# Second half of x by block transposes, the residual's moves from ScalarE's queue, and the rest group ahead of the last late blocks

## The chip, the cores and the metric

The kernel runs on one core of a Trainium2 chip. A core has a matrix engine (TensorE, PE in the profile, with its weight loads as PEld), a vector engine (VectorE, DVE), a scalar engine (ScalarE, ACT), a general engine (GpSimd, POOL) and a sync engine (SyncE, SP). SP and ACT can both issue transfers (DMAs), and each engine works off its own instructions in order and waits for the others by semaphores. The metric is the device time of one execution in microseconds (us); smaller is better.

## The reference

Two blocks follow each other on 8 batches of 576 tokens, all in 32-bit floats. The first is attention with 8 heads of width 64 in which only scores within `tau` of the row's maximum are kept. The second is a mixer: a small network over the tokens, added to x, then one over the channels, added to that.

```
# q, k, v: (8, 8, 576, 64); w_tok1 (576, 256), w_tok2 (256, 576), w_ch1 (512, 1536), w_ch2 (1536, 512)
scores = scale * q @ k^T
scores = where(scores >= max(scores) - tau, scores, -1e9)
attn = exp(scores - max(scores)); attn /= sum(attn) + 1e-9
x = (attn @ v), heads side by side: (8, 576, 512)

h  = relu(x^T @ w_tok1) @ w_tok2          # over tokens
u  = x + h^T
h2 = relu(u @ w_ch1) @ w_ch2              # over channels
out = u + h2
```

## The kernel before

**How the work is cut.** A batch is called a row here, 0 to 7. Its 8 heads are 4 pairs, and two pairs side by side (a "quad", 4 heads, 256 of the 512 channels) are worked through in nine units of 128 query rows. Two units make a score round (`scores_of_two`, L848), after which DVE takes the maximum (`top`, L865), POOL makes the bias (`shift`, L871), ACT masks and takes exponentials (`mask`, L881, and `exps`, L891), DVE inverts the sums (L277, L278), POOL scales (`scale`, L286), DVE transposes in blocks of 32 by 32 (`turn_blocks`, L316), and four DMAs per unit put the blocks in place (`move`, L328). After three units PE multiplies by v (`values`, L366 and L371). Its result is copied to `xT` (L375), which holds x with the channels on the partitions.

**x with tokens on the partitions.** The token network needs x the other way round, in `x_sb`. For rows 1 to 7 this is done in two ways. The first quad, ready half a row early, goes through `early_x`: two DVE block transposes (L398) into a tile `xs`, then four DMAs of 128 KB on SP (L411), then the last 64 tokens in the same manner (L405, L418). The second quad goes through PE: `turn_x` (L441) transposes four 128x128 blocks into a PSUM bank, twice, and a third time for the last 64 tokens; ACT or DVE copies each bank to `x_sb` (L445). The columns that the DMA way leaves are in another order of blocks, and `tok1` (L460) reads the first quad through a rearranged view.

**The token network.** `tok1` multiplies `w1` by x, in two steps per row, ReLU follows (L470 or L473); `tok2` (L478) multiplies by `w2`, and `add_x` (L489) adds into `xT`.

**The channel network.** Each row has two groups of 256 tokens and a rest of 64. The list `NOW` says how many groups of a row run during the attention: both of row 0, one each of rows 1 to 6, none of row 7. Such a group has 12 first-layer steps (`ch1`, L1058, ReLU at L1063 on ACT or L1066 on DVE) and, but for row 0's first, seven products in place of eight (`make_seven`, L982), the sums for which are taken on DVE and POOL. The residual u is needed there with the tokens on the partitions: `turn_u` (L1043) transposes it in blocks on DVE, and `move_u` (L1050) issues 4 moves of two DMAs each, on SP's queue, into `ut`. Seven groups do so.

**What is put off.** The other groups run after the attention, as "late" blocks of 512 tokens (class `Late`, products at L1430): two groups per block, the last of these being both groups of row 7, and as a fifth block the eight rests of 64 tokens. Rows 0 to 6 are kept in device memory meanwhile (`spill`, L537) and loaded again (L1447). A late block has seven products at each of two levels, so that its second half is a net of sums on DVE and POOL. For each of two halves m (128 tokens of either group t), a fifth product (`x5`) is added into two of the four output parts. The outputs go to memory by `store` (L1455), four stores per block, all on SP; in the block of rests each store is two DMAs of 64 tokens.

**What sets the order.** All instructions are placed by a planner written in the kernel (`Scheduler`). An operation has an engine, a cost in us, dependencies and a rank; the planner keeps a clock for each engine, places what can start first, and the engines then keep this order. Two PSUM banks serve everything but the scores until the attention ends, eight after that. A DMA is modelled with its issue time, its size, and at most eight in flight. A score round of row 1 and later is held back while the planned PE work of the token and channel networks is behind `planned_at`: the more is subtracted there (`KEEP`, for the second to last row `KEEP_LAST`), the earlier the round may run.

The few lines that steer this before the change:

```
KEEP, KEEP_LAST = 24.0, 26.0
...
return total + part * (k - 2) / (UB // 2) - (KEEP_LAST if row == B - 2 else KEEP)
...
groups.append([(b, 2 * GR, REST) for b in range(B)])
```

## Time and profile before

| what | us |
|---|---|
| median of 3 runs (1227.75 to 1229.17) | 1227.9 |
| the profiled execution | 1229.4 |
| its span, first to last instruction | 1227.6 |
| attention with rows 0 to 7 woven in | to about 862 |
| five late blocks (products L1430) | 864 to 1220 |

The profile is of one execution. Its span leaves out 1.8 us that the device time holds around it. A row of the attention takes about 98 us in the middle of the kernel. Between 272 and 770 us, PE is busy 99% of the time, DVE 73%, ACT 56%, POOL 35%, and the 16 transfer engines some 70 to 78%. The granted TensorE clock is 0.997 of full speed in the mean.

A group line of the page names the code line, the engine, the operation, output and input, how often, the busy time and the mean of one; a wait line names who waited for whom. PE's matmuls overlap, so a matmul's own duration is longer than the step from one start to the next: a first-layer step of the channel network (8 records) takes 1.75 us from start to start.

### The profile page before, as it was taken

How to read it: one execution, taken by the hardware profiler on the slowest of the kernel's cores; microseconds unless marked ns; L12 is line 12 of the kernel's file. 1: busy time of each engine (PE TensorE's matmuls, PEld its weight loads, DVE VectorE, ACT ScalarE, POOL GpSimd, SP SyncE). 2: the span in 40 equal slices, each digit the busy share in tenths (PEclk: the TensorE clock that was granted, in tenths of full speed). 3: DMA queues.
4: the chain of work that ended last, by engine and by line, in shares of the span. 5: the costliest groups of instructions: out<-in, count | busy, mean ns of one | idle time of the engine just before them, and what ended most of it. 6: DMA issues, size and time to landing. Idle time of an engine off the chain costs nothing.

```text
span 1227.6 us, 21546 instructions
## 1 busy us (share of the span) xinstructions
PE 1199.0 (98%) x7769; PEld 972.6 (79%) x7769; DVE 877.8 (71%) x1406; ACT 572.6 (47%) x1279; POOL 365.7 (30%) x568
## 2 busy tenths in 40 slices
PE   9888999999999999999999999999999999999996
PEld 8655788777777777876877777788899898999986
DVE  6798996777778668776867766843767575766756
ACT  6987863555663665574555456530211212121220
POOL 3666552333343423332433323411001010110101
PEclk9999999999999999999999999999999999999999
DMA  8656867767778757877767687661211202020101
GB/s 145 140 121 163 234 169 169 153 145 179 175 161 185 174 124 178 182 158 168 161 153 168 151 183 152 151 165 34 52 35 47 58 18 53 1 69 1 54 17 35
DMA packets 325370, 149.76 MB, mean 122 GB/s; under 512 B 223824, under 2 KB 318032, under 8 KB 325264
## 3 DMA queue, kind: packets, MB, share of 16 engines
q1 hardware_dynamic: 323392, 148.17, 52.9%
q8 instruction: 62, 1.02, 0.3%
q10 hardware_dynamic: 1872, 0.21, 0.1%
q14 instruction: 44, 0.36, 0.1%
HBM read 47.32 MB, written 13.50 MB: 50 GB/s over the span
## 4 chain that ended last, share of the span: by engine, by line
PE 85%; DVE 2%; DMA 0%; ACT 0%; issue 0%; SPq 0%; DVEq 0%
PE bank L1430 28%; PE bank L1058 12%; PE bank L982 11%; PE sc L848 10%; PE bank L371 8%; PE bank L460 5%; PE bank L478 5%; PE bank L366 3%; PE bank L1073 2%; DVE mx L865 1%; PE bank L441 0%; DVE us L946 0%; DVE g L1066 0%; DMA lk<-in_k_dram 0%; ACT e L881 0%
## 5 line engine op out<-in xcount | busy, mean ns | idle before, releaser
L881 ACT ACTIVATE e<-sc,bias 128x576 f32<-128x576 f32 x288 | 194.3, 742 | 173.1 <-POOL bias L871 171.9
L286 POOL TENSOR_SCALAR e<-e,rr 128x576 f32<-128x576 f32 x288 | 216.6, 769 | 189.3 <-DVE rr L278 187.8
L891 ACT ACTIVATE e<-e,ntau 128x576 f32<-128x576 f32 x288 | 220.8, 780 | 0.2
L865 DVE TENSOR_REDUCE mx<-sc 128x2 f32<-128x1152 f32 x144 | 188.1, 1348 | 40.5 <-PE sc L848 39.8
L316 DVE STREAM_TRANSPOSE T<-e 128x1152 f32<-128x1152 f32 x126 | 171.0, 1365 | 31.0 <-POOL e L286 21.8
L1058 PE MATMUL bank<-xT,wc 128*128 128x256 f32 x768 | 177.1, 383 | 1.9 <-ACT g L1063 0.9
L848 PE MATMUL sc<-kT,qT 64*128 64x192 f32 (+1 forms) x1920 | 165.5, 333 | 1.0 <-ACT e L881 1.0
L1058 PEld LDWEIGHTS bank<-xT,wc 128*128 128x128 f32 x768 | 143.0, 190 | 28.9 <-issue 4.4
L848 PEld LDWEIGHTS sc<-kT,qT 64*128 64x128 f32 (+1 forms) x1920 | 138.4, 176 | 31.2 <-issue 19.3
L371 PE MATMUL bank<-eT,lv 128*64 128x384 f32 (+1 forms) x1024 | 135.1, 406 | 0.0
L371 PEld LDWEIGHTS bank<-eT,lv 128*64 128x64 f32 x1024 | 73.7, 137 | 50.5 <-issue 44.3
L871 POOL TENSOR_SCALAR bias<-mx,toff 128x2 f32<-128x2 f32 x144 | 39.3, 273 | 193.1 <-DVE mx L865 186.0
L946 POOL TENSOR_TENSOR us<-us,late_x 128x256 f32<-128x256 f32 x14 | 13.1, 934 | 219.9 <-DVE us L946 156.9
L982 PE MATMUL bank<-wc,g 128*128 128x256 f32 x336 | 77.8, 381 | 0.0
L478 PE MATMUL bank<-w,a 128*128 128x192 f32 (+1 forms) x256 | 74.4, 425 | 1.2 <-DVE xT L489 0.7
L460 PE MATMUL bank<-x_sb,w 128*128 128x256 f32 x320 | 73.0, 383 | 0.7 <-DVE x_sb L445 0.5
L982 PEld LDWEIGHTS bank<-wc,g 128*128 128x128 f32 x336 | 63.1, 190 | 12.8 <-issue 2.5
L460 PEld LDWEIGHTS bank<-x_sb,w 128*128 128x128 f32 x320 | 59.8, 190 | 10.9 <-issue 1.1
L478 PEld LDWEIGHTS bank<-w,a 128*128 128x128 f32 x256 | 43.6, 192 | 22.5 <-issue 6.4
L1430 PE MATMUL bank<-t,w1s 128*128 128x256 f32 x240 | 60.8, 379 | 0.0
L946 DVE TENSOR_TENSOR temps<-bank,temps 128x256 f32<-128x256 f32 x60 | 25.3, 422 | 49.5 <-PE bank L1430 47.1
L1430 PE MATMUL bank<-t,wc 128*128 128x256 f32 x240 | 59.2, 379 | 0.0
(175 smaller groups left out, 1820.0 us busy)
## 6 DMA issues: line engine op xcount, KB each, us to landing
eT<-T SPq DMA_DIRECT2D x504, 144.0 KB, 3.0
w2s<-in_moe_w_ch_dram SPq DMA_DIRECT2D x24, 512.0 KB, 4.2
lk<-in_k_dram SPq DMA_DIRECT2D x122, 72.0 KB, 2.9
ut<-us SPq DMA_DIRECT2D x136, 64.0 KB, 2.1
lq<-in_q_dram SPq DMA_DIRECT2D x120, 72.0 KB, 3.1
out_dram<-us SPq DMA_DIRECT2D x32, 256.0 KB, 2.1
lv<-in_v_dram SPq DMA_DIRECT2D x112, 72.0 KB, 2.5
spill<-xT SPq DMA_DIRECT2D x6, 640.0 KB, 4.0
```

Of the source, the lines that this page charges most:

```text
L286: nc.gpsimd.tensor_scalar(out=eh, in0=eh, scalar1=rr[:, h : h + 1], scalar2=1.0, op0=ALU.mult, op1=ALU.mult)
L316: nc.vector.transpose(out=T.rearrange("p a (c x) -> p c a x", c=NK), in_=e.rearrange("p (c a x) -> p c a x", c=NK, a=4))
L371: nc.tensor.matmul(to[r], lhsT=lv[:, j, :], rhs=e[j], start=False, stop=(c == NI - 1), skip_group_check=True)
L460: nc.tensor.matmul(to, lhsT=w1[:, t, P * m : P * m + P], rhs=x(t), start=(t == 0), stop=(t == NT - 1), skip_group_check=len(products) > 1,)
L478: nc.tensor.matmul(bank[:, n * i : n * i + n], lhsT=hidden[b][:, m, P * c : P * c + P], rhs=w2[:, m, lo : lo + n], start=(m == 0), stop=(m ...
L848: nc.tensor.matmul(sc[h][rows, f, HT * k : HT * k + HT], lhsT=qT[r, cols], rhs=kT[r, HT * f : HT * f + HT], start=True, stop=True, skip_gr ...
L865: nc.vector.tensor_reduce(out=mx[:, h], in_=sc[h][:, :, 0 : 2 * HT].rearrange("p f (k x) -> p k f x", k=2), axis=AX.XY, op=ALU.max)
L881: nc.scalar.activation(out=eh, in_=part[h], func=AF.Prelu, bias=bias[:, h], scale=SCALE, alpha=STEEP)
L891: nc.scalar.activation(out=eh, in_=eh, func=AF.Exp, bias=ntau, accum_out=rs[:, h, 0:1])
L982: nc.tensor.matmul(bank[:, 0:HD], lhsT=x[:, j, :], rhs=y[:, j, :], start=j == 0, stop=j == HJ - 1)
L1058: nc.tensor.matmul(bank[:, 0:n], lhsT=wc1[:, j, c, :], rhs=uT[:, c, GR * i : GR * i + n], start=(c == 0), stop=(c == NCC - 1))
L1430: nc.tensor.matmul(to, lhsT=l, rhs=r, start=start and x == 0, stop=x == len(pairs) - 1, skip_group_check=not start)
```

## The change

- `early_x` takes the first pair `c0` as an argument and is called for the second quad of rows 1 to 7 as well, without its last 64 tokens. `turn_x` has only these 64 tokens left in those rows. `tok1` reads the second quad's main part through a rearranged view too. The moves are ranked ahead of the other transfers in the planner.
- `move_u` issues on ACT's queue, with rank 3 in place of 1 and a modelled issue time of 0.55 us.
- `KEEP` and `KEEP_LAST` go from 24 and 26 us to 14 and 20.
- The block of rests is put in the third place of the five; row 7's block is the last.
- In the last block (`ends`), the fifth products come after the inner ones, their addends are prepared by an addition on POOL or DVE, and the stores of the second group (t = 1) go to ACT's queue.

```
-    def early_x(b):
+    def early_x(b, c0):
...
-                in_=xT[:, c, 0:MAIN].rearrange("q (t r a) -> q t a r", t=NI, a=4),
+                in_=xT[:, c0 + c, 0:MAIN].rearrange("q (t r a) -> q t a r", t=NI, a=4),
...
-                out=x_sb[:, 0:NI, 32 * HQ * i : 32 * HQ * i + 32 * HQ],
+                out=x_sb[:, 0:NI, P * c0 + 32 * HQ * i : P * c0 + 32 * HQ * i + 32 * HQ],
...
-        for t, n in [(t, n) for t in range(0, NI, n)] + [(NI, 1)]:
+        for t, n in [(t, n) for t in range(0, NI, n) if not b] + [(NI, 1)]:
...
-    KEEP, KEEP_LAST = 24.0, 26.0
+    KEEP, KEEP_LAST = 14.0, 20.0
...
+        moved = [sched.op("sp", 1.2, lambda i=i: move_main(i), turns + before, -1 if c0 else 0, dmas=(1, 131, 0.69)) for i in range(4)]
+        if not c0:
+            last = sched.op("dve", 0.35, turn_rest, moved, 2)
...
-                    nc.sync.dma_start(
+                    eng.dma_start(
                         out=s["ut"][:, m, k, :], in_=s["us"][32 * k : 32 * k + 32, m]
...
-                moved = [sched.op("sp", 1.2, lambda k=k, m=move_u: m(k), (turn,), 1, dmas=(nt, 64, 0.69)) for k in range(4)]
+                moved = [sched.op("act", 1.2, lambda k=k, m=move_u: m(k, nc.scalar), (turn,), 3, dmas=(nt, 64, 0.55)) for k in range(4)]
...
+        while late_due and key_op("V", rank_of_group(late_due[0], HQ, 2)).end is not None:
+            make_early(late_due.pop(0), HQ)
...
-    groups.append([(b, 2 * GR, REST) for b in range(B)])
+    groups.insert(2, [(b, 2 * GR, REST) for b in range(B)])
...
+            ends = self.n == len(groups) - 1
+            for m in range(0 if ends else 2):
                 x5 = plain(lambda m=m: sum_place(0, m), lambda: w2s[:, 0], [s1[m]])
...
+                if ends:
+                    b11 = on_pool(lambda eng, m=m: add(old(1, 1, m), old(1, 1, m), four(w7_of(m)), eng), [u3] + moved[m])
+                    x5 = plain(lambda m=m: sum_place(0, m), lambda: w2s[:, 0], [s1[m]] + small_used[0] + small_used[1][:1])
+                    q11 = put_mid("dve", 0.42, lambda bank, m=m: add(four(o(1, 1, m)), four(bank), old(1, 1, m)), x5, [x5, b11])
+                    q01b = put_leave("dve", 0.42, lambda bank, m=m: add(o(0, 1, m), bank[:, 0:HD], o(0, 1, m)), x5, [x5, q11, q01b])
...
+                    if ends and t:
+                        x = sched.op("act", 0.53, lambda m=m, t=t, rows=rows: self.store(2 * t + m, rows(), nc.scalar), deps, 1)
```

More of the change, by code (lines that the diff above doesn't have):

```diff
@@ L454, in tok1 @@
             else:
-                first = lambda t: x_sb[:, t, 0 : P * HQ].rearrange("p (i c d) -> p c i d", i=4, c=HQ)
-                products = [(slice(0, P * HQ), first), (to_cols, lambda t: x_sb[:, t, to_cols])]
+                blocks = lambda t, c0: x_sb[:, t, P * c0 : P * c0 + P * HQ].rearrange("p (i c d) -> p c i d", i=4, c=HQ)
+                products = [
+                    (slice(0, P * HQ), lambda t: blocks(t, 0)),
+                    (to_cols, lambda t: blocks(t, HQ) if t < NI else x_sb[:, t, to_cols]),
+                ]
             for at, x in products:
@@ L927, with make_early @@
     early = {}
-    def make_early(b):
-        turn_main, turn_rest, move_main, move_rest = early_x(b)
-        have = [key_op("X", rank_of_group(b, 0, g)) for g in range(3)]
-        free = early.get(b - 1, []) + [x for k, x in keyed.items() if k[0] == "tok" and k[1] == b - 1 and len(k) == 3]
+    def make_early(b, c0=0):
+        turn_main, turn_rest, move_main, move_rest = early_x(b, c0)
+        have = [key_op("X", rank_of_group(b, c0, g)) for g in range(3)]
+        free = early.get(b if c0 else b - 1, []) + [x for k, x in keyed.items() if k[0] == "tok" and k[1] == b - 1 and len(k) == 3]
         turns = [sched.op("dve", 1.1, lambda c=c: turn_main(c), have + free, 2) for c in range(HQ)]
         before = [x for k, x in keyed.items() if k[0] == "tok" and k[1] == b - 1 and len(k) == 3 and x.first_layer]
-        moved = [sched.op("sp", 1.2, lambda i=i: move_main(i), turns + before, 0, dmas=(1, 131, 0.69)) for i in range(4)]
-        last = sched.op("dve", 0.35, turn_rest, moved, 2)
-        moved += [sched.op("sp", 0.6, lambda i=i: move_rest(i), [last] + before, 0, dmas=(1, 16, 0.6)) for i in range(4)]
-        early[b] = moved
-        xreads.setdefault(b, []).extend(turns + [last])
+        moved = [sched.op("sp", 1.2, lambda i=i: move_main(i), turns + before, -1 if c0 else 0, dmas=(1, 131, 0.69)) for i in range(4)]
+        if not c0:
+            last = sched.op("dve", 0.35, turn_rest, moved, 2)
+            moved += [sched.op("sp", 0.6, lambda i=i: move_rest(i), [last] + before, 0, dmas=(1, 16, 0.6)) for i in range(4)]
+            turns.append(last)
+        early[b] = early.get(b, []) + moved
+        xreads.setdefault(b, []).extend(turns)
     def side2(k, n):
@@ L1046, in turn_u, with move_u @@
                     )
-            def move_u(k, s=s):
+            def move_u(k, eng, s=s):
                 for m in range(nt):
-                    nc.sync.dma_start(
+                    eng.dma_start(
                         out=s["ut"][:, m, k, :], in_=s["us"][32 * k : 32 * k + 32, m]
@@ L1267, in make_round @@
                 if t // GU == 2:
-                    (rows_due if p0 == NP - 2 else early_due).append(b)
-    rows_due, early_due = [], []
+                    (late_due if p0 else early_due).append(b)
+                    if p0:
+                        rows_due.append(b)
+    rows_due, early_due, late_due = [], [], []
     def planned_at(row, k):
@@ L1448, in load, with store @@
                 at += n
-        def store(self, t, rows):
+        def store(self, t, rows, eng=None):
             at = 0
@@ L1454, in store @@
                 if first < last:
-                    nc.sync.dma_start(
+                    (eng or nc.sync).dma_start(
                         out=out[b, lo + first - at : lo + last - at, :], in_=rows[first - P * t : last - P * t]
@@ L1613, in make_second @@
                 s4[m] = sched.op("dve", 0.96, lambda m=m: sub(a(0, 1, m), a(0, 1, m), sum_place(1, m)), [s2[m], x2[m]], 2)
-            for m in range(2):
+            ends = self.n == len(groups) - 1
+            for m in range(0 if ends else 2):
                 x5 = plain(lambda m=m: sum_place(0, m), lambda: w2s[:, 0], [s1[m]])
@@ L1626, in make_second @@
                 u2 = on_pool(lambda eng, m=m: add(w6_place(m), w6_place(m), p1_place(m), eng), w6[m] + [c1[m]], rank=2)
-                q01a = on_pool(lambda eng, m=m: add(four(o(0, 1, m)), four(o(0, 1, m)), old(0, 1, m), eng), w3[m] + [y5b[m]])
+                q01a = on_pool(lambda eng, m=m: add(four(o(0, 1, m)), four(o(0, 1, m)), old(0, 1, m), eng), w3[m] + [y5b[m]] + moved[m])
                 q01b = on_pool(lambda eng, m=m: add(o(0, 1, m), o(0, 1, m), w6_place(m), eng), [q01a, u2])
@@ L1631, in make_second @@
                 q10b = on_pool(lambda eng, m=m: add(o(1, 0, m), o(1, 0, m), w7_of(m), eng), [q10a, u3])
-                q11 = on_pool(lambda eng, m=m: add(o(1, 1, m), o(1, 1, m), w7_of(m), eng), [y5[m], u3])
+                if ends:
[3 more added lines that the diff above has]
+                    q01b = put_leave("dve", 0.42, lambda bank, m=m: add(o(0, 1, m), bank[:, 0:HD], o(0, 1, m)), x5, [x5, q11, q01b])
+                else:
+                    q11 = on_pool(lambda eng, m=m: add(o(1, 1, m), o(1, 1, m), w7_of(m), eng), [y5[m], u3])
                 self.outs[m] = [q00, q01b, q10b, q11]
@@ L1635, in make_second @@
                     count = 2 if len(groups[self.n]) > 2 else 1
-                    self.stores[m].append(
-                        sched.op("sp", 0.6, lambda m=m, t=t: self.store(2 * t + m, self.us[m][:, t].rearrange("q a x -> q (a x)")), deps, 1, dmas=(count, 256 // count, 0.6))
-                    )
+                    rows = lambda m=m, t=t: self.us[m][:, t].rearrange("q a x -> q (a x)")
+                    if ends and t:
+                        x = sched.op("act", 0.53, lambda m=m, t=t, rows=rows: self.store(2 * t + m, rows(), nc.scalar), deps, 1)
+                    else:
+                        x = sched.op("sp", 0.6, lambda m=m, t=t, rows=rows: self.store(2 * t + m, rows()), deps, 1, dmas=(count, 256 // count, 0.6))
+                    self.stores[m].append(x)
                 all_second += self.outs[m]
```

## The prediction

> **What bounds the kernel now.** I read the page's busy shares and its chain of waits first, then the busy time by stretches, then the waits of TensorE (PE), then single stretches of the timeline around the edited steps.

> ```profile
> PE 1199.0 (98%) x7769; PEld 972.6 (79%) x7769; DVE 877.8 (71%) x1406; ACT 572.6 (47%) x1279; POOL 365.7 (30%) x568
> ...
> PE 85%; DVE 2%; DMA 0%; ACT 0%; issue 0%; SPq 0%; DVEq 0%
> ```

> The chain that ends last is PE work. The stretches (columns: length, then busy us of PE, weight loads, DVE, ACT, POOL, clock, DMA share, GB/s) say where PE is not full:

> ```profile
> 0.00:120.00 120.00, 106.14 (x837) 78.59 (x838) 97.12 (x169) 99.73 (x209) 68.60 (x111) 0.99 0.66 140
> 120.00:260.00 140.00, 137.69 (x978) 110.20 (x977) 113.20 (x160) 87.83 (x192) 58.30 (x82) 1.00 0.75 178
> ...
> 680.00:820.00 140.00, 139.93 (x908) 109.08 (x904) 101.64 (x136) 72.91 (x160) 47.10 (x78) 1.00 0.72 161
> ...
> 1150.00:1200.00 50.00, 50.00 (x257) 44.63 (x255) 30.54 (x60) 11.72 (x30) 2.43 (x3) 1.00 0.15 43
> 1200.00:1228.00 28.00, 17.95 (x144) 16.99 (x142) 17.91 (x43) 1.59 (x6) 4.93 (x7) 0.90 0.17 38
> ```

> From 120 to 1200 us PE idles about 5 us in all. Only the start (14 us idle) and the end (10 us idle) hold more. So a microsecond of PE work removed in the middle is a microsecond gained, as long as nothing new makes PE wait; and the last 28 us are a stage of their own, where DVE and the stores set the end.

> **The transposes that go.** Rows 1 to 7 lose two PE transpose steps each (four 128x128 transposes into one bank, L441, then a copy, L445). Two of them in the timeline:

> ```profile
> 630.35 0.66 PE L441 MATMUL bank<-ident,xT 128*128 128x128 f32 x4
> 630.84 1.89 PE L1058 MATMUL bank<-xT,wc 128*128 128x256 f32 x8
> 632.57 0.60 PE L441 MATMUL bank<-ident,xT 128*128 128x128 f32 x4
> 633.46 1.99 PE L1058 MATMUL bank<-xT,wc 128*128 128x256 f32 x8 [0.29 <-DVE g L1066]
> ```

> A step's price is the time from its start to the next instruction's start, 0.49 and 0.89 us here (the second holds a bank wait of 0.29). Eight such steps, near 333, 531, 631 and 826 us, sum to 4.85 us with the waits and 4.28 without: 0.61 or 0.54 each. Fourteen steps are 8.5 or 7.5 us; I take **-8.0**. The built order of the changed kernel has 56 transposes fewer and every other PE instruction in the same number, so this part is certain. Fourteen copies of 0.58 us (ACT) or 0.68 us (DVE) go too, off the path.

> **What brings x instead.** Per row two block transposes on DVE and four 128 KB moves on SP. The first quad already does this, so its rows price it:

> ```profile
> 280.98 0.56 DVE L375 COPY xT<-bank 128x384 f32<-128x384 f32 x1 [1.02 <-PE bank L371]
> ...
> 282.94 2.16 DVE L398 STREAM_TRANSPOSE xs<-xT 128x512 f32<-128x512 f32 x2
> ```
> ```profile
> 285.74 2.87 SPq L411 DMA_DIRECT2D x_sb<-xs  x4
> ```
> ```profile
> DMA to landing us min/median/max: 2.8/3.3/4.3
> ```

> From the end of the values product (280.9) to the last landing (285.7+2.9+3.3 = 291.9) is 11.0 us. What lies in front of the first layer's second half in the changed order, from the row's last values product on, with the durations of before (ch1 step L1058 1.75, score round 2.15 or 2.3, seven-product L982 2.6, remaining transposes 0.3, values 3.3, and the first layer's own first half 2.2): row 1 has 11.6 us, row 4 12.4, row 7 10.2, rows 2, 3, 5 and 6 at least 17. In row 7 the attention is over and DVE and SP stand free, so its chain is 0.6+2.2+2.5+3.3 = 8.6 us. So x arrives about as it is needed: I take **+1.0** for all rows. Lower bound 0. Upper bound: a maximum pair lies in front on DVE (2.6 us, L865) and eight eT moves on SP (5 us). Then the chain is 18.6 us in rows 1 and 4, and 11.2 in row 7, where only DVE's 2.6 can be: 7.0, 6.2 and 1.0 late, 14 us. The 11.0 us already hold some such queueing (1.4 us before the turn, 0.6 before SP), so I don't count both in both rows and use +9. DVE gains 14 x 1.11 = 15.6 us in some 740 us where it is 73% busy, and SP 28 x 0.63 = 17.7 us.

> [...]

> **The residual's moves.** Seven groups issue four moves of two DMAs each (L1050): 56 issues of 0.60 us leave SP and go to ACT. SP wins 34 us and, with the 18 added, is 16 us lighter; nothing on PE waits for SP's issue time alone, so no gain. ACT, 56% busy there, is held while it issues: the five ACT issues at the start took 0.36 to 0.58 us each, SP's 0.60, so a block of eight is about 4.8 us. Each issue also waits for the DVE turn and for transfers further up. Queued behind it on ACT are the ch1 ReLUs that free PE's two banks and the masks of the next round. In the built order three ch1 steps (5.2 us) beside such a block in row 0 drain through DVE, and a score round (2.15) follows: 7.4 us of cover for 4.8. I take **+1.5** in all; bounds 0 and +7 (1 us in each group). If the cover were gone, a block would cost its 4.8 us.

> **The lead.** The planner's lead falls from 24 to 14 us, so more of the older rows' products run before a score round. That moves PE work, it makes none; as five idle us are spread over 1080, I put 0 (-1 to +3).

> **The late blocks.** The rest group now comes third. Its eight loads (8 x 0.6 us issue, 3.2 us landing) come a group ahead, and a late group lasts about 70 us: 0. The last group is now a pair of whole blocks, and its two fifth products (six 128x256 matmuls, 2.6 us each) run at the very end. The end today:

> ```profile
> 1215.90 0.83 PE L1430 MATMUL bank<-late_x,hidden_b 128*128 128x128 f32 x6
> ...
> 1216.57 0.83 PE L1430 MATMUL bank<-wc,ga 128*128 128x128 f32 x6
> ...
> 1218.01 6.79 SPq L1455 DMA_DIRECT2D out_dram<-us  x8
> ...
> 1219.02 0.91 PE L1430 MATMUL bank<-wc,hidden_b 128*128 128x128 f32 x6 [1.61 <-DVE us L946]
> ...
> 1221.84 0.42 DVE L946 TENSOR_TENSOR us<-us,late_x 128x256 f32<-128x256 f32 x1
> ```

> PE waits 1.6 us for DVE, DVE ends at 1222.26, and SP, which issues eight 128 KB stores at 0.6 us, starts the last at 1224.2; it lands 2.4 us later and the span ends 1.0 after that. Now: without the 5.2 us of fifth products the inner chain comes 5.1 us earlier (DVE had 5.3 us idle in it), PE reaches 1217.4 at 1212.3, does the first fifth product to 1214.9, the last inner one to 1215.6, the second fifth one to 1218.2. DVE's adds, 1.5 us more of them, run along to 1218.0; the two on the last bank end at 1219.3, 3.0 earlier than 1222.3. One 256 KB store on each queue is then left (2.1 us to landing), so 1.9 us of queue and 0.3 of landing go too: **-5.1**. Bounds: -1.5 if DVE can't come forward and only the store queue's gain stays, -6.5 if the first gap closes too.

> **Sum.** -8.0 + 1.0 + 1.5 - 5.1 = -10.6 us. The profiled execution took 1229.4 us (span 1227.6 and 1.8 around it): 1218.8. The median of the runs, 1227.9, lies 1.5 below that, so **1217.3 us**.

> **Rivals.**
> - *x comes late.* The 11 us chain meets DVE and SP as busy as in the bound above: +9 for +1, about 1225. For it: row 1 and 4 have only 0.6 and 1.4 us to spare, and SP issues about 0.6 us apiece almost without pause. Against it: four of seven rows have 6 us more.
> - *The end is DVE's.* DVE is busy 17.9 of the last 28 us, ends after PE, and gets 1.5 us more; the fifth products then only fill waits, the tail gives -1.5: about 1221. Against it: its 5.3 idle us just before.
> - *Slower: ACT is held by its DMA issues.* One block of eight per group, seven times. Past 7.4 us of cover, an issue of 1.3 us (SP's slowest for these moves was 1.6) makes a block 10.4 us and PE loses 3.0 us seven times, 21 in place of 1.5: about 1237. It decides from 12.1/7 = 1.7 us lost per group, an issue of (7.4+1.7)/8 = 1.14 us. For it: the issues wait on transfers already in flight. Against it: SP's median for the very same moves, 0.60.
> - That the transposes stay is excluded by the built order.

> **How the numbers follow.** Forecast 0.55, x late 0.20, the end 0.15, ACT held 0.10. Below 0.2% (2.5 us), which is about what this kernel's timing can tell from no change, lies only an edge of x late. Faster 0.87, same 0.03, slower 0.10. The range 1211 to 1227 reaches from both best ends (-8.5, -6.5, 0, -1) to x late; it leaves out ACT held and the edges. The forecast's own range is 1212 to 1221.

> **What would show it.** PE's matmul records fall by 56, L441's 128x128 group from 72 to 16. PE's waits between 120 and 860 us stay under 8 us; a wait of the first layer (L460 before) for a DMA, or of ch1 for an ACT ReLU, would name the first or third rival. The last matmul ends near 1218.2 - 8.0 + 2.5 = 1212.7 with no PE gap over 1 us ahead of it, then comes one store per queue, and the span ends within 5 us. It is wrong if PE's idle time in the attention grows by more than 8 us.

## The result, and the profile after

The changed kernel takes 1242.1 us in the median of six runs (1238.3 to 1243.5), the kernel before 1227.9 on the same chips: 1.0105 times as long (95% interval 1.0086 to 1.0124), some 13 us slower. The profiled execution took 1238.3 us, the fastest of the six, with a span of 1236.5: the trace holds 9 us of the loss. The six runs go with the granted clock, 0.995 of full speed in the two fastest and 0.991 to 0.993 in the others.

The page's busy shares, and the first line of its chain of waits:

```profile
PE 1195.5 (97%) x7713; PEld 967.7 (78%) x7713; DVE 887.6 (72%) x1414; ACT 567.6 (46%) x1271; POOL 371.1 (30%) x568
...
PE 71%; DVE 5%; DMA 5%; SPq 4%; ACT 2%; issue 1%; ACTq 1%; POOL 0%; DVEq 0%; POOLq 0%
```

The matmul records fell by 56, as they had to, but PE's busy time fell by 3.5 us only (1199.0 to 1195.5), where 8 was forecast. And the chain that ends last, 85% PE before, now runs through DVE, transfers and SP's queue in 14% of the span. The stretches (length, then busy us of PE, weight loads, DVE, ACT, POOL, then PE's clock, DMA share, GB/s) say where:

```profile
120.00:260.00 140.00, 138.39 (x951) 110.17 (x949) 105.50 (x149) 82.47 (x182) 54.33 (x73) 1.00 0.72 172
...
400.00:540.00 140.00, 135.59 (x918) 105.08 (x918) 100.43 (x141) 76.20 (x170) 49.98 (x82) 1.00 0.78 170
540.00:680.00 140.00, 133.16 (x844) 101.26 (x842) 99.58 (x136) 73.70 (x158) 45.85 (x78) 0.98 0.77 168
680.00:820.00 140.00, 136.70 (x923) 102.50 (x920) 103.64 (x144) 76.64 (x172) 50.42 (x83) 1.00 0.72 165
820.00:880.00 60.00, 55.17 (x271) 44.25 (x270) 27.95 (x38) 9.69 (x23) 12.29 (x10) 0.97 0.35 94
...
1200.00:1237.00 37.00, 31.61 (x223) 29.34 (x221) 29.13 (x58) 3.74 (x14) 6.27 (x8) 0.96 0.08 29
```

From 120 to 900 us PE idles 21.2 us (the 780 us less its busy time), before 5.1. The late products run without a break from 880.7 us on, in place of 864.3; as one late step of 2.6 us has already run by then, the attention takes 13.8 us longer. The rest, to the end of the span, takes 358.4 us with that step, in place of 363.3: 4.9 us less. So the loss is all in the attention, and the tail gave what was forecast.

**Two of the long waits.** The first is 5.65 us, in row 5. From the timeline (start, length, engine, line and operation, and in brackets the idle time before with what ended it):

```profile
599.98 2.23 DVE L1048 STREAM_TRANSPOSE us<-xT 128x512 f32<-128x512 f32 x2
...
602.24 1.86 ACTq L1055 DMA_DIRECT2D ut<-us  x3
...
603.34 4.88 SPq L411 DMA_DIRECT2D x_sb<-xs  x4
...
611.35 0.31 DVE L405 STREAM_TRANSPOSE xs<-xT 128x128 f32<-128x128 f32 x1 [9.14 <-DMA x_sb<-xs]
...
611.84 0.53 DVE L375 COPY xT<-bank 128x384 f32<-128x384 f32 x1
...
612.42 4.21 PE L1063 MATMUL bank<-xT,wc 128*128 128x256 f32 x9 [5.65 <-DVE xT L375]
```

The one waited for is not the second quad's x. DVE stands 9.14 us at L405, the turn of the first quad's last 64 tokens, which waits for that quad's moves. These start at 603.34 on SP, which had issued nothing since 596.1. What SP waited for stands in the list of its queue's waits, with the total in us, how often, and the longest:

```profile
SPq L411 <- DMA ut<-us: 9.3, 3, 7.2
```

A move of x waits 7.2 us for a transfer of the residual, which it does not read. In this trace the landings of all 1193 transfers of SP and ACT are told on the same eight semaphores, 100 to 107, and no transfer was issued before the one ahead of it on its semaphore had landed. The move of x at 603.34 is on 102, and so is the one ahead of it, the first of ACT's residual moves, which follow the turn at 599.98: issued at 601.18, it lands at 603.27. SP waits for 102 until then. Behind L405, in DVE's order, stands the copy that frees PE's bank, and PE stops.

The clock makes this wait dearer. The same stretch in steps of 2 us (columns as above, the clock is the third number from the end):

```profile
606.00:608.00 2.00, 0.77 (x10) 0.47 (x6) 0.00 (x0) 0.00 (x0) 0.00 (x0) 1.00 0.65 136
608.00:610.00 2.00, 0.00 (x0) 0.00 (x0) 0.00 (x0) 0.00 (x0) 0.00 (x0) 0.93 0.83 152
610.00:612.00 2.00, 0.00 (x0) 0.00 (x0) 0.61 (x4) 0.00 (x0) 0.00 (x0) 0.50 0.89 146
...
614.00:616.00 2.00, 2.00 (x7) 1.55 (x6) 0.99 (x1) 0.00 (x0) 1.03 (x2) 0.50 0.77 187
```

PE is back at 612.4 and runs at a clock of 0.50 until 616.5, half of which, some 2 us, is lost on top of the wait. The second wait is in row 7, before the last first-layer products:

```profile
852.73 0.69 DVE L954 TENSOR_TENSOR t<-u 128x512 f32<-128x512 f32 x1 [6.51 <-PE bank L987]
...
854.67 2.09 DVE L398 STREAM_TRANSPOSE xs<-xT 128x512 f32<-128x512 f32 x2
...
856.79 3.04 SPq L411 DMA_DIRECT2D x_sb<-xs  x4
...
862.12 4.08 PE L463 MATMUL bank<-x_sb,w 128*128 128x256 f32 x10 [4.83 <-DMA x_sb<-xs]
```

Here it is the second quad's x. The late blocks' sums (L954) are placed ahead of its turn, and they wait for a load of u from device memory. The bracket names PE, but the chain of waits (start, length, what) goes back from the turn to this load:

```profile
847.59 4.93 DMA u<-spill
```

From the turn's start to PE's is 7.5 us; x is late because its turn starts late.

**The tail.** The last matmuls, stores and sums:

```profile
1228.96 2.76 PE L1439 MATMUL bank<-w2s,x_sb 128*128 128x256 f32 x12
...
1230.10 2.51 ACTq L1464 DMA_DIRECT2D out_dram<-us  x2
...
1231.86 1.02 SPq L1464 DMA_DIRECT2D out_dram<-us  x2
...
1232.09 0.41 DVE L951 TENSOR_TENSOR us<-bank,us 128x256 f32<-128x256 f32 x1
```

PE has no wait in the last 40 us, the two queues store side by side, and the span ends 4.8 us after the last matmul.

### The profile page after: what moved, and what is told of

Its sections match the earlier page's. It is cut to its first block, busy times and chain, and to the rows that moved or that the text cites. A ratio compares the mean times of both kernels' runs of the same rounds, so it can differ in the third digit from the quotient of the medians.

```text
span 1236.5 us, 21484 instructions
## 1 busy us (share of the span) xinstructions
PE 1195.5 (97%) x7713; PEld 967.7 (78%) x7713; DVE 887.6 (72%) x1414; ACT 567.6 (46%) x1271; POOL 371.1 (30%) x568
## 3 DMA queue, kind: packets, MB, share of 16 engines
HBM read 47.32 MB, written 13.50 MB: 49 GB/s over the span
## 4 chain that ended last, share of the span: by engine, by line
PE 71%; DVE 5%; DMA 5%; SPq 4%; ACT 2%; issue 1%; ACTq 1%; POOL 0%; DVEq 0%; POOLq 0%
PE bank L1439 28%; PE bank L987 9%; PE sc L851 8%; PE bank L1063 7%; PE bank L371 7%; PE bank L463 5%; PE bank L481 3%; PE bank L366 2%; PE bank L1078 2%; SPq L328 2%; DMA ut<-us 1%; DVE T L316 1%; DMA eT<-T 1%; DVE mx L868 1%; SPq L128 1%
## 5 line engine op out<-in xcount | busy, mean ns | idle before, releaser
L316 DVE STREAM_TRANSPOSE T<-e 128x1152 f32<-128x1152 f32 x126 | 170.5, 1363 | 32.6 <-POOL e L286 16.9
L371 PE MATMUL bank<-eT,lv 128*64 128x384 f32 (+1 forms) x1024 | 135.2, 406 | 0.0
L371 PEld LDWEIGHTS bank<-eT,lv 128*64 128x64 f32 x1024 | 74.5, 137 | 49.7 <-issue 41.1
L1068 ACT ACTIVATE g<-bank 128x256 f32<-128x256 f32 x55 | 21.3, 387 | 117.3 <-PE bank L1063 114.8
L463 PEld LDWEIGHTS bank<-x_sb,w 128*128 128x128 f32 x320 | 61.0, 193 | 17.4 <-issue 7.7
L481 PE MATMUL bank<-w,a 128*128 128x192 f32 (+1 forms) x256 | 71.3, 418 | 1.4 <-DVE xT L492 0.9
L987 PEld LDWEIGHTS bank<-wc,g 128*128 128x128 f32 x336 | 63.2, 190 | 12.1 <-DVE mx L868 1.2
L481 PEld LDWEIGHTS bank<-w,a 128*128 128x128 f32 x256 | 43.3, 189 | 22.4 <-issue 6.8
```

The source lines that it names most:

```text
L316: nc.vector.transpose(out=T.rearrange("p a (c x) -> p c a x", c=NK), in_=e.rearrange("p (c a x) -> p c a x", c=NK, a=4))
L371: nc.tensor.matmul(to[r], lhsT=lv[:, j, :], rhs=e[j], start=False, stop=(c == NI - 1), skip_group_check=True)
L463: nc.tensor.matmul(to, lhsT=w1[:, t, P * m : P * m + P], rhs=x(t), start=(t == 0), stop=(t == NT - 1), skip_group_check=len(products) > 1,)
L481: nc.tensor.matmul(bank[:, n * i : n * i + n], lhsT=hidden[b][:, m, P * c : P * c + P], rhs=w2[:, m, lo : lo + n], start=(m == 0), stop=(m ...
L987: nc.tensor.matmul(bank[:, 0:HD], lhsT=x[:, j, :], rhs=y[:, j, :], start=j == 0, stop=j == HJ - 1)
```

## The experiments

Several readings stood against one another: that the residual's moves hold ScalarE and its queue (theory 1 in the first expectations), that x by transfers comes late (2), that the shorter lead costs (3), and that any other order of the planner's is worse than the one before (4). Later runs narrowed this to three, which their expectations call A (the load of the moves on SP and the transfer engines), B (x's own way) and C (the planner's order). The table has all runs but the one with pauses at the end; "to before" is the ratio less 1, times 1228 us. Idle is 780 us less PE's busy time from 120 to 900 us, and "clock" what PE's busy time there lost to the lowered clock (half of the time at 0.50). Both are from one profiled execution, which lay up to 5 us from its kernel's median. Differences between two rows' ratios carry some 2 us of noise either way.

| run | median us | ratio (95%) | to before, us | idle, us | clock, us |
|---|---|---|---|---|---|
| before | 1227.9 | | | 5.1 | 0 |
| change | 1242.1 | 1.0105 (1.0086, 1.0124) | +12.9 | 21.2 | 3.8 |
| change, residual's moves on SP | 1238.9 | 1.0078 (1.0052, 1.0105) | +9.6 | 16.9 | 7.8 |
| change, lead 24/26 | 1244.5 | 1.0115 (1.0091, 1.0139) | +14.1 | 24.6 | 6.4 |
| change, second quad on PE | 1244.6 | 1.0112 (1.0084, 1.0139) | +13.8 | 16.8 | 3.4 |
| late blocks alone | 1224.9 | 0.9953 (0.9938, 0.9969) | -5.8 | 5.1 | 0 |
| late + lead 14/20 | 1228.3 | 0.9996 (0.9986, 1.0006) | -0.5 | 6.8 | 0 |
| late + lead 22/24 | 1226.3 | 0.9981 (0.9970, 0.9991) | -2.3 | 5.5 | 0 |
| late + residual's moves on ACT | 1231.9 | 1.0027 (1.0015, 1.0038) | +3.3 | 9.5 | 1.7 |
| late + x by transfers | 1245.4 | 1.0134 (1.0117, 1.0151) | +16.5 | 22.1 | 10.6 |
| late + moves that nobody reads | 1243.0 | 1.0123 (1.0107, 1.0139) | +15.1 | 16.2 | 4.2 |
| late + x, its moves on ACT | 1245.2 | 1.0142 (1.0125, 1.0159) | +17.4 | 23.7 | 4.9 |
| rests third only | 1226.8 | 0.9984 (0.9975, 0.9994) | -2.0 | 5.6 | 0 |
| unread moves counted, not issued | 1241.8 | 1.0110 (1.0095, 1.0125) | +13.5 | 16.0 | 4.4 |
| unread moves issued, not counted | 1228.4 | 0.9997 (0.9987, 1.0007) | -0.4 | 8.3 | 0 |
| late + x, moves not counted | 1222.5 | 0.9950 (0.9936, 0.9965) | -6.1 | 9.5 | 0 |
| change, x's moves not counted | 1230.0 | 1.0012 (1.0002, 1.0022) | +1.5 | 14.6 | 1.7 |
| change, no moves counted | 1234.0 | 1.0043 (1.0027, 1.0059) | +5.3 | 16.5 | 3.0 |
| the same, lead 24/26 | 1255.1 | 1.0217 (1.0200, 1.0234) | +26.6 | 27.8 | 7.7 |

### One part undone, and the tail alone

The residual's moves back on SP:

```
-                moved = [sched.op("act", 1.2, lambda k=k, m=move_u: m(k, nc.scalar), (turn,), 3, dmas=(nt, 64, 0.55)) for k in range(4)]
+                moved = [sched.op("sp", 1.2, lambda k=k, m=move_u: m(k, nc.sync), (turn,), 1, dmas=(nt, 64, 0.69)) for k in range(4)]
```

> The changed kernel with only the residual's moves put back on SP's queue (rank 1, 0.69 us as before). Theory 1 (the moves on ACT cost the time: SP and ACT transfers wait for each other's completion in one order, so that a late ACT move holds SP, then DVE, then PE): PE's idle time between 120 and 880 us falls from 21 to under 8 us, 1219 to 1225 us. Theory 2 (x by DMA comes too late, whoever moves the residual): 1234 to 1242, with waits for x_sb and DVE as now. Theory 3 (the lead of 14 us is too short): 1234 to 1242.

1238.9 us, idle 16.9, so theory 1 alone is not enough. The 5.65 us wait behind L405 is gone, but others came: 4.03 us at 341, 3.05 at 545 and 2.87 at 749, all of score rounds that follow one another with little between. The clock falls to 0.50 after each of the three, and its dips cost 7.8 us more.

The lead of before:

```
-    KEEP, KEEP_LAST = 14.0, 20.0
+    KEEP, KEEP_LAST = 24.0, 26.0
```

> The changed kernel with only the lead put back to 24 and 26 us. Theory 3 (lead): 1219 to 1226 us. Theories 1 and 2: 1234 to 1244, with PE waits over 1.5 us for DVE or for DMAs left in the attention.

1244.5 us, idle 24.6, with 6.54 us for x before 868.1 as the longest wait. The lead alone is not the cause.

The second quad's x on PE again, the rest as changed:

```
-                    (to_cols, lambda t: blocks(t, HQ) if t < NI else x_sb[:, t, to_cols]),
+                    (to_cols, lambda t: x_sb[:, t, to_cols]),
...
-        for t, n in [(t, n) for t in range(0, NI, n) if not b] + [(NI, 1)]:
+        for t, n in [(t, n) for t in range(0, NI, n)] + [(NI, 1)]:
...
-        while late_due and key_op("V", rank_of_group(late_due[0], HQ, 2)).end is not None:
-            make_early(late_due.pop(0), HQ)
```

> The changed kernel with the second quad's x back on PE (14 transpose steps more, 8 us of PE work); the moves on ACT, the lead of 14 and the late blocks as changed. Theory 2 (x by DMA): PE's idle time in the attention falls under 8 us, and the time is that of before less the tail's 5 us: 1222 to 1226. Theory 1 (moves on ACT) and theory 3 (lead): stalls of 8 us and more stay and the 8 us of transposes come on top of the tail's gain: 1231 to 1242.

1244.6 us, idle 16.8, above all that was expected: no better without any of the new moves of x. The waits are at still other places (2.5 us for v at 538, 2.2 at 851). So no single part, taken away, gives the time back.

The late blocks alone on the kernel before (all three edits above together):

> The kernel before with only the late blocks changed (rests third, row 7's block last, its fifth products at the end, stores on two queues). All theories: the attention as before, the end 5 us sooner: 1222 to 1224 us, PE idle in the attention about 5 us.

1224.9 us, 0.9953, faster than both kernels. The tail's gain is 5.8 us by the ratio, and idle time is 5.1 us as before.

### One part added to the late blocks

Each is the last kernel with one part of the change: the lead of 14/20, x by transfers, or the residual's moves on ACT (the lines above the other way round), and as a control a lead of 22/24.

> The kernel before with the late blocks changed and the lead at 14 and 20 us; x of the second quad on PE, the moves on SP. Theory 3 (the short lead leaves nothing to run beside a wait): PE idle in the attention 12 us or more, 1231 to 1242. Theories 1 and 2: idle under 8 us, 1221 to 1226. Theory 4 (any change of the planned order loses, because the order of before is an unusually good one): 1229 to 1242.

> The kernel before with the late blocks changed and the second quad's x by DMA; lead 24 and 26, the moves on SP. Theory 2 (x by DMA is itself late): PE waits for x_sb or for DVE behind it, 1229 to 1242. Theories 1 and 3: the transposes' 8 us are gained, 1213 to 1220. Theory 4: 1227 to 1240.

> The kernel before with the late blocks changed and the residual's moves on ACT's queue; lead 24 and 26, x on PE. Theory 1 (moves on ACT): ACT or SP held at each other's transfers, PE idle in the attention 12 us or more, 1231 to 1244. Theories 2 and 3: 1222 to 1226. Theory 4: 1229 to 1242.

> A control: the kernel before with the late blocks changed and the lead moved by 2 us only (22 and 24); x on PE, the moves on SP. Theories 1 to 3: as with the late blocks alone, 1223 to 1227. Theory 4 (the order of before is a lucky one and its neighbours are worse): 1229 us or more, with PE waits spread over several kinds.

The run with x by transfers took 1245.4 us, above all that was expected. Against the late blocks alone, by the ratios: lead +5.3, x by transfers +22.2, the moves on ACT +9.1, all three together +18.7. The sum of the parts would be +36.6, so they do not add. The control, which only shifts when score rounds run by 2 us, is 3.4 us slower by the ratios, little beyond the noise; its 1226.3 us lie where theories 1 to 3 put it and short of the 1229 of theory 4. The lead alone, at 1228.3, fell between the ranges.

The moves on ACT alone make one queue wait for the other, as in the change. The longest PE wait is for a load of v, and SP waits for transfers of the residual, as it does nowhere in the late blocks alone (a line of PE's timeline, then one of the list of SP's waits):

```profile
622.44 1.50 PE L366 MATMUL bank<-eT,vl 128*64 128x384 f32 x4 [1.94 <-DMA lv<-in_v_dram]
SPq L328 <- DMA ut<-us: 13.8, 8, 3.6
```

The load of v stands on SP behind a move of `eT` that ACT's moves had held for 2.9 us. PE's waits for ACT's ReLUs are 0.9 us, as without these moves.

x by transfers is the dearest. As its transposes (6 to 8 us) are gone, its waits are worth some 28 to 30, which the trace bears out: 17.0 us more idle and 10.6 us at the lowered clock. The longest is 6.75 us at 540: PE waits for `eT`, whose eight moves are issued from 534.8 on, behind loads and other moves that SP issues from 518.8 on almost without a pause. That spoke for the load on SP's queue, and the next runs test it. Two more are for x itself, 3.15 us before 764.2 and this one:

```profile
647.53 1.71 PE L463 MATMUL bank<-x_sb,w 128*128 128x256 f32 x5 [3.46 <-DMA x_sb<-xs]
```

From the end of the values product (637.5) to x's landing it is 10.0 us, about the chain that the prediction added up; this order has only 6.6 us of PE work in front of it.

### Load, way or order

Moves that nobody reads: x on PE, and in rows 1 to 7 four moves as large and as finely cut as those of x, from a weight tile to a scratch tile in device memory. (The page has 17.17 MB written there in place of 13.50; x's own moves write none.) This is added work; `[...]` stands for the rearranged views.

```
+    spare = dram.tile([P, NI, 4, 64], F32, name="spare")
+    def make_spare(b):
+        have = [key_op("X", rank_of_group(b, HQ, g)) for g in range(3)]
+        for i in range(4):
+            sched.op("sp", 1.2, lambda i=i: nc.sync.dma_start(out=spare[...], in_=wc2[...]), have + converted, -1, dmas=(1, 131, 0.69))
```

> The late blocks alone, with x on PE, and in rows 1 to 7 four more 128 KB moves in 256 B pieces on SP's queue, issued where the change issues its moves of x, from a weight tile into a scratch tile that nobody reads. They add SP's issue time and the transfers' load, but nobody needs their data and DVE turns nothing for them (added work: 28 transfers). Theory A (the load on SP's queue delays everything behind it, eT above all): PE's idle time from 120 to 900 us rises from 4.8 us to 12 us or more, and the time lies at 1238 us or above. Theory B (only x's own way, turn, move and landing, has no work of PE to hide behind): idle time stays below 8 us, and the time is within 3 us of the late blocks alone, 1224.9.

1243.0 us, idle 16.2. B falls as the main cause: x itself has its old way here and the loss is nearly the same. Taken alone this says A.

x by transfers, its moves issued by ACT:

```
-        moved = [sched.op("sp", 1.2, lambda i=i: move_main(i), turns + before, -1 if c0 else 0, dmas=(1, 131, 0.69)) for i in range(4)]
+        if c0:
+            moved = [sched.op("act", 0.6, lambda i=i: move_main(i, nc.scalar), turns + before, -1, dmas=(1, 131, 0.55)) for i in range(4)]
```

> Late blocks and x by transfers (lead 24/26, the residual's moves on SP), but the second quad's four moves of x are issued by ACT in place of SP. Theory A (SP's queue): SP is relieved of 28 issues, the waits for V <- eT and score rounds go, PE's idle time from 120 to 900 us falls from 22 us to below 10, and the time falls from 1245.4 to 1220 to 1228. Theory B (x's own way): x takes the same 10 us or more to arrive, idle time stays at 15 us or more, and the time stays at 1238 us or above.

1245.2 us, idle 23.7: relieving SP of these issues gained nothing. But SP was not free either, as its queue now waits for x's moves on ACT, at six places 22.4 us in all (none with the moves on SP):

```profile
SPq L328 <- DMA x_sb<-xs: 17.4, 5, 7.7
```

So this run does not decide on A, and the next two do.

The built order of the run with unread moves gave the hint: it differs from that of the late blocks alone on PE too, with score rounds side by side and the channel products, which filled the time between them, in one piece later. The planner has the moves in its model of SP and the transfers. So it was split: moves counted but never issued (the same order, none of the load), and issued but not counted (the order of the late blocks alone, all of the load; the 28 moves are added work).

```
-                lambda i=i: nc.sync.dma_start(out=spare[...], in_=wc2[...]),
+                lambda: None,
```

> The kernel with the unread moves again, but the 28 moves are only counted by the planner and never issued: all other instructions keep that kernel's order, and the added load is gone. Theory C (the planner's order: with four more moves in its model it bunches the work that should fill the score chain, so that rounds stand back to back): the time stays at 1236 us or above, with the same waits near 676 and 688 us and 10 us or more idle from 120 to 900 us. Theory A (the load of the moves on SP and the transfer engines): the time returns to 1222 to 1228 us.

```
-                1.2,
+                0.0,
...
-                dmas=(1, 131, 0.69),
```

> The late blocks alone, in their own order, with the 28 unread moves of 128 KB issued on SP at the same places but counted as nothing by the planner: the load is there, the order is not changed. Theory C (order): within 3 us of the late blocks alone, 1222 to 1228 us, idle below 8 us. Theory A (load): 1236 us or above, idle 12 us or more.

Counted but not issued: 1241.8 us, with the same waits. Issued but not counted: 1228.4, at the edge of what C expected, with 3.2 us more idle than the late blocks alone and no loss to the clock. On PE, DVE, ACT and POOL every instruction stands in the order of the run with unread moves in the first, and in that of the late blocks alone in the second. The order alone accounts for 19.3 us against the late blocks alone (1.0110 against 0.9953), the load alone for 5.4. The two orders around the same score rounds, from PE's timeline, first counted and not issued:

```profile
664.30 2.22 PE L851 MATMUL sc<-kT,qT 64*128 64x192 f32 x24
666.45 2.86 PE L481 MATMUL bank<-w,a 128*128 128x384 f32 x12
669.69 1.57 PE L481 MATMUL bank<-w,a 128*128 128x192 f32 x8 [0.38 <-DVE xT L492]
671.19 2.82 PE L851 MATMUL sc<-kT,qT 64*128 64x192 f32 x36
679.27 1.55 PE L366 MATMUL bank<-eT,vl 128*64 128x384 f32 x4 [5.26 <-DMA eT<-T]
...
685.46 2.22 PE L851 MATMUL sc<-kT,qT 64*128 64x192 f32 x24
690.89 0.59 PE L851 MATMUL sc<-kT,qT 64*128 64x192 f32 x2 [3.21 <-ACT e L884]
```

And issued, not counted:

```profile
671.91 2.38 PE L851 MATMUL sc<-kT,qT 64*128 64x192 f32 x36
674.22 1.56 PE L481 MATMUL bank<-w,a 128*128 128x384 f32 x4
675.62 2.75 PE L1003 MATMUL bank<-wc,g 128*128 128x256 f32 x12
678.30 0.87 PE L366 MATMUL bank<-eT,vl 128*64 128x384 f32 x4
...
683.17 2.22 PE L851 MATMUL sc<-kT,qT 64*128 64x192 f32 x24
685.32 1.57 PE L481 MATMUL bank<-w,a 128*128 128x192 f32 x8
686.73 2.75 PE L1003 MATMUL bank<-wc,g 128*128 128x256 f32 x12
```

In the second, token products (L481) and one of the seven channel products (L1003) lie behind each score round while its maximum, exponentials, turns and moves run. In the first, nothing lies between the round at 671 and the values at 679, and two rounds stand side by side at 685 and 691.

Then with x: late blocks and x by transfers, every turn and move of it issued, but in the model the second quad's moves cost SP nothing and land 4 us after they start.

```
-        moved = [sched.op("sp", 1.2, lambda i=i: move_main(i), turns + before, -1 if c0 else 0, dmas=(1, 131, 0.69)) for i in range(4)]
+        if c0:
+            moved = [sched.op("sp", 0.0, lambda i=i: move_main(i), turns + before, -1, lag=4.0) for i in range(4)]
```

> Late blocks and x by transfers (lead 24/26, the residual's moves on SP) as in the run that took 1245.4 us, with all the same turns and moves of x issued, but in the planner's model the second quad's moves cost nothing on SP and land 4 us after their start. Its order stays as regular as that of before: after each row's first score round the two remaining transposes and products of the channel network, no score rounds back to back. Theory C (order): most of the 22 us idle goes, idle below 10 us, and the transposes' 8 us show: 1217 to 1226 us. Theory B (x's own way is too long, whatever the order): idle of 15 us or more, 1238 us or above. Between them the two share it.

1222.5 us, in place of 1245.4: 22.6 us gone by the ratios, with every DVE turn and every transfer of x still there. Only the planner's model differs, so this is the price of the order with x in place. (The order is nearer to that of the late blocks alone, but not the same.) PE's busy time is 1192.3 us, 6.2 below the late blocks alone. The group of the first layer's matmuls, with what it waited for at its end:

```profile
L463 PE MATMUL bank<-x_sb,w 128*128 128x256 f32 x320 | 73.0, 383 | 1.9 <-DMA x_sb<-xs 1.1
```

PE waits 1.1 us in all for x. Yet idle time is 9.5 us in place of 5.1, so of the 6.2 us some 1.8 are left, and the ratio is that of the late blocks alone within its interval.

### The change with its moves uncounted

The same edit in the whole change, then the residual's moves on ACT uncounted as well, then that with the lead of 24/26:

```
-                moved = [sched.op("act", 1.2, lambda k=k, m=move_u: m(k, nc.scalar), (turn,), 3, dmas=(nt, 64, 0.55)) for k in range(4)]
+                moved = [sched.op("act", 0.0, lambda k=k, m=move_u: m(k, nc.scalar), (turn,), 3, lag=4.0) for k in range(4)]
```

> The whole changed kernel (lead 14/20, the residual's moves on ScalarE's queue), but the planner counts nothing for the second quad's moves of x and takes them as landed 4 us after their start. If the order that these moves brought about is what cost most (theory C), most of the 14 us between the changed kernel and the kernel before goes: 1224 to 1231 us, 8 to 13 us idle from 120 to 900 us, the rest being the lead and the moves on ScalarE. If the lead and the moves on ScalarE weigh as much within the change, 1236 us or above.

> As the run before, and the residual's moves on ScalarE's queue count as nothing either (landed 4 us after the start). If those moves cost by the planner's order too, 3 to 6 us less than the run before; if by holding ScalarE for their issue and coupling the two queues, the same or more.

> As the run before with the lead of 24/26 us. Its order is the most regular one with x by transfers: after each row's first score round the remaining transposes, products of the channel network and the first layer, and a fill between all rounds. Theory C: idle from 120 to 900 us below 10 us and 1216 to 1223 us, below both kernels. If the moves on ScalarE's queue hurt by themselves, 1226 us or more.

Without x's moves in the model the change takes 1230.0 us, as expected: 11.4 us less by the ratios, though the 14.6 us idle are more than expected. Leaving ACT's moves out too is worse, 1234.0, and with the longer lead 1255.1, the slowest of all, although that order looked the most regular; I had expected 1216 to 1223. The last one's timeline shows a part of why:

```profile
825.96 6.70 ACTq L1059 DMA_DIRECT2D ut<-us  x8
...
827.66 1.99 PE L1067 MATMUL bank<-xT,wc 128*128 128x256 f32 x8
...
832.70 0.54 ACT L375 COPY xT<-bank 128x192 f32<-128x192 f32 x2 [7.95 <-DMA ut<-us]
833.29 1.99 PE L1067 MATMUL bank<-xT,wc 128*128 128x256 f32 x8 [3.64 <-ACT xT L375]
```

Eight residual moves hold ACT for 6.7 us, 0.84 each. The two copies that free PE's banks stand behind them, and PE waits 3.64 us after one product. Uncounted, such waits for ACT come at 428, 534, 734 and 833 us, 9.9 of the 27.8 us idle. The two longest are others, 5.81 us for `eT` before 329.0 and 5.48 for x before 857.9, and were not followed further. So leaving a move out of the model is no remedy as such.

### The tail's parts, and the price of a wait

The block of rests third, with nothing else changed from before:

```
-    groups.append([(b, 2 * GR, REST) for b in range(B)])
+    groups.insert(2, [(b, 2 * GR, REST) for b in range(B)])
```

> Before, with the block of rests in third place only: no fifth products at the very end, all stores on SP. By the prediction's parts of the tail the store queue's share stays (the last stores are four 256 KB ones in place of eight 128 KB ones, and all on SP): about -1.5 us, 1226.4. The fifth products' share of -3 and the second queue's go. Rival: the tail's gain is all the change of order, then 1222 to 1225 as with the late blocks alone.

1226.8 us, about as expected, -2.0 by the ratio, so the later fifth products and the second queue give the other 3.8 of 5.8.

Pauses of rising length behind the late blocks' kernel (added work):

```
+    for k in (1, 2, 3, 4, 5, 6, 7, 8):
...
+        for _ in range(100):
+            nc.tensor.transpose(out=pause[:, 0:P], in_=x_sb[:, 0, 0:P], identity=ident)
+        nc.vector.tensor_copy(out=x_sb[:, 1, 0:P], in_=pause[:, 0:P])
+        for i in range(k):
+            nc.vector.tensor_copy(out=x_sb[:, (i + 2) % 3 + 1, :], in_=x_sb[:, (i + 1) % 3 + 1, :])
+        nc.vector.tensor_copy(out=x_sb[:, 0, :], in_=x_sb[:, k % 3 + 1, :])
```

> The late blocks alone, and after the kernel's own end eight pauses of PE of rising length: 100 transposes of 128x128, then a chain of 3 to 10 copies on DVE (about 0.7 us each) that PE waits for, then 100 transposes again. This adds work of 120 to 150 us and measures the price of a wait by itself. Theory of the clock: after waits of under about 2.5 us the granted clock stays at 1.0, after waits of over about 3.5 us it falls to 0.5 for 4 to 5 us, which costs 2 to 2.5 us on top of the wait. Rival: the dips in the kernels belong to contention or to the thin work after the wait; then 100 transposes take the same time after every pause.

```profile
1242.78 11.14 PE L1729 MATMUL pause<-ident,x_sb 128*128 128x128 f32 x100 [1.51 <-DVE x_sb L1733]
1255.89 12.81 PE L1729 MATMUL pause<-ident,x_sb 128*128 128x128 f32 x100 [1.97 <-DVE x_sb L1733]
1271.13 11.13 PE L1729 MATMUL pause<-ident,x_sb 128*128 128x128 f32 x100 [2.44 <-DVE x_sb L1733]
1285.17 11.14 PE L1729 MATMUL pause<-ident,x_sb 128*128 128x128 f32 x100 [2.90 <-DVE x_sb L1733]
1299.66 12.80 PE L1729 MATMUL pause<-ident,x_sb 128*128 128x128 f32 x100 [3.36 <-DVE x_sb L1733]
1316.29 13.59 PE L1729 MATMUL pause<-ident,x_sb 128*128 128x128 f32 x100 [3.82 <-DVE x_sb L1733]
```

In this one execution the same 100 transposes take 11.1 us after waits of 1.05, 1.51, 2.44 and 2.90 us, 12.8 after 1.97, 3.36 and 4.28, and 13.6 after 3.82: where a wait costs more than its length, it is 1.7 to 2.5 us more. The 2.5 and 3.5 us of the expectation, and its 4 to 5 us at 0.50, were an estimate that this run does not show: 1.97 us cost 1.7 more and the longer 2.44 and 2.90 us nothing, so the length alone does not decide. The last section has where the waits fell.

## Why the prediction was wrong, point by point

- **The transposes, -8.0.** Right in kind, somewhat large: with x's moves uncounted PE's busy time falls by 6.2 us. In the change it falls by 3.5 only, the half-speed stretches being part of that time.
- **x by transfers, +1.0: "So x arrives about as it is needed."** The size holds where x's moves are not counted (1.1 us of waits). The chain is nearly right too: its 11.0 us count the landing from the end of the last issue, and the trace has that move landed at 291.31, so 10.4. But the cover was read from one order only, and with x by transfers alone the planner left 6.6 us in front of such a chain. Moves of this size issued for nobody, though into device memory, cost 5.4 us by their load, which had no term: "SP ... is 16 us lighter; nothing on PE waits for SP's issue time alone" let SP's extra moves pass for free. In the change itself x's wait comes where DVE is held ahead of its turn (row 7). In the change the moves of 128 KB land in 3.1 us in the median, where 3.3 was counted.
- **The residual's moves, +1.5.** Mis-sized and with the wrong mechanism: +9.1 by the ratios, at or past the upper bound of +7. The sum and the rival "ACT is held" both priced the time in which ACT issues. But an issue takes 0.61 us in the median, below the 1.14 from which that rival was to decide, and with these moves alone PE waits no longer for ACT's ReLUs. What I had not named is the other queue: SP's transfers wait for landings of ACT's on a semaphore that both use, 23 us in all in the change and 20 with the moves alone, and PE waits for what stands behind them. ACT's hold shows on PE too, but less: in the change a block keeps ACT from its exponentials from 803.3 to 807.0 us and PE waits 2.09 us before 811.7, and the last uncounted run has the 3.64 us shown above. How much of the 9.1 is the order was not split off.
- **The lead, 0.** Mis-sized: +5.3 alone, by the ratios at or past its bound of +3; in the traces the late blocks start 4.9 us later. With x by transfers in SP's model the shorter lead helps instead: 16.5 against 9.6 us above before.
- **The tail, -5.1, and the rests third, 0.** Right: 4.9 us in the trace, 5.8 by the late blocks alone. PE has no gap over 1 us there, and the span ends 4.8 us after the last matmul.
- **The step that failed** is one under all of these: the sum prices each edit at the place where the work of before stood, and takes the order from the built kernel only to count cover for x and for ACT's issues. It has no term for the order. But this planner sets the whole order anew from its model, and "That moves PE work, it makes none" is not harmless where the work moved is the fill behind score rounds. Shown for moves that nobody reads: 19.3 us by the order alone; for x by transfers, 22.6. Within the change, leaving x's moves out of the model takes 11.4 of its 18.7 us above the late blocks alone. The other 7.3 are lead, ACT's moves and x together and were not taken apart.
- **The price of a wait.** All waits were priced at their length. The change's 16.1 us of added idle time and the 3.8 us lost to half clock after the two longest waits, less the 6.2 of the transposes, make 13.7 of the 13.8 us that the attention lost.
- **The rivals.** "It is wrong if PE's idle time in the attention grows by more than 8 us": it grew by 16.1. "x comes late" named a wait that is there (4.83 us in row 7), but that is under a third of the idle time added, and the rival still gave a gain. The slow rival had the right sign by another way, and its 1237 comes near by luck.

What stays open: why counting x's moves leads to a worse order. In the model they delay what stands behind them on SP, but which decision tips was not traced. Nor is it shown that any order with them must be bad: the change without x by transfers was as slow as with it, so the order of before may also simply be a good one. The control with a lead of 22/24 lost only some 3.4 us, so not every other order is as bad.

The best version here has the late blocks, x by transfers with its moves uncounted, and the residual's moves on SP: 0.9950 (0.9936 to 0.9965) of before. It cannot be told from the late blocks alone, 0.9953.

## What to carry to other kernels

Where a planner sets the order, an edit is two changes, the work and the order; price the order apart, by reading in the built kernel what fills PE behind each long chain, and test it by counting work that is not issued and issuing work that is not counted. A queue's issue time is not free because nobody waits for the queue as such (28 moves that nobody reads cost 5.4 us here by their load): name the next transfer on it, what in-order engine waits for that, and what stands behind that. A PE wait can be dearer than its length: among the pauses here one of 1.97 us cost 1.7 us more, and one of 2.90 us nothing more.

## What was not expected of the hardware

```profile
1256.00:1256.50 0.50, 0.50 (x6) 1.00 0.00 0
1256.50:1257.00 0.50, 0.50 (x5) 0.51 0.00 0
```

PE had been back at work since 1255.89. Steps of 3.413 us, counted off from these falls, sort the pauses. The wait of 1.97 us lay inside one step (1253.10 to 1256.51), and the clock fell at its end. The waits of 2.44 and 2.90 us were cut by the end of a step, into 1.5 and 1.0 and into 1.6 and 1.3 us, and cost nothing. Among the pauses, at full clock, steps with up to 1.73 us of idle time were not followed by a fall, and those with 1.97 us and more all were. From 120 to 900 us of the other runs the line is less sharp, but near there: the least idle time before a fall is 1.87 us, the most without one 1.99. Earlier, near 107 us, some falls followed 1.5 us, so idle time as this trace has it does not decide alone. What else does was not shown.
